# A searched-on instruction order: 110 further seeds for the planner of an attention, gated-mixer and token-mixer kernel

## The chip, the core and the metric

The kernel runs on one core of a Trainium2 chip. The metric is the device time of one launch in microseconds (us); lower is better. Engines are named as the profile names them: PE (TensorE; PEld are its weight loads), ACT (ScalarE), DVE (VectorE), POOL (GpSimd), SP (SyncE, which issues nearly all DMAs).

## The reference

Three stages follow each other, all in fp32, for 4 batches of 448 tokens with 768 features.

```python
q_n, k_n = rmsnorm(q, g_q), rmsnorm(k, g_k)          # 12 heads of 64
scores = q_n @ k_n.T / 8 ;  attn = exp(scores - max) ;  attn /= attn.sum() + 1e-9
x = attn @ v                                          # [4, 448, 768]
h = relu(x @ w_in) ;  u, v = halves of h              # 2 x 512
v_n = (v - mean) / sqrt(var + 1e-6)
x = (u * (w_spatial @ v_n + b_spatial)) @ w_out       # mixes over tokens
u = x + (relu(x.T @ w_tok1) @ w_tok2).T               # 448 -> 256 -> 448 over tokens
out = u + relu(u @ w_ch1) @ w_ch2                     # 768 -> 1536 -> 768
```

## The kernel before

**What runs when.** The 48 heads are taken as 24 pairs. For one pair, `Attention.slot` loads q and k (`load`), scales them on POOL (`scale`, output tile `raw`), turns them with PE (`transposed`), multiplies them (`scores`, PSUM tile `sc`), takes the row maximum on DVE (`nm`) and the exponential on ACT (`e`), turns `e` with PE (`turned`, PSUM tile `tp`, copied to `et`) and multiplies it with v (`values`, PSUM tile `av`). The row sums go another way: DVE adds 1e-9, inverts and transposes them (`divisors`, tiles `ring` and `rows`), SP writes them to DRAM (`over_d<-rows`) and reads them back spread over 64 partitions each (`over<-over_d`). DVE multiplies `av` with `over`, ACT rounds the product to its high part and POOL takes the low part (both in tile `xp`). A batch has six pairs, and when its six `xp` are there, `moe` computes the mixer: `vps` (v, six `xp` by w_in), `ups` (u), `sps` (over tokens), `xps` (w_out). Its weights come through DRAM; ACT, DVE, POOL and SP prepare them on the way (`word`, `wpart`, `wv`, `wu_d`, `stage`, `ws`). After the last batch come the token mixer (`h1ps`, `u_ps`, transposes of `x`) and the channel mixer in seven products each way (`h2ps`, `o_ps`).

Most matmuls take the operands as a high and a low fp32r part and run three passes. In the first eight pairs the scores take fp32 whole (`sc<-whole`), later three fp32r passes (`sc<-kt,qt`).

**What sets the order.** Nothing is issued while the loops run. `Plan.add` records each operation with its operands, a cost and its dependencies. At the end `Plan.issue` lays all recorded operations out by a list scheduler, `Plan.place`: on each engine the ready operation of the lowest weight goes first, with the PSUM banks given out as they come free, and the operations are then issued engine by engine in the order of the starts that it found. The weights come from eight rounds forward and back. They are then changed by a list of seeds:

```python
for seed in NUDGES:
    weight = nudged(weight, seed, engines)
start, span, bank = self.place(prev, succ, lag, weight, (opens, closes, users))
```

`nudged` turns a seed into a place in the program (modulo `NUDGED`, 4000), a reach, a size and a kind (all engines or one), and adds to the weights of the operations around that place a pseudo-random amount. So a seed moves no more than some operations against their neighbours; what is computed, with which tiles, stays. Which bank a PSUM tile takes follows the order as well. Before the change the list holds 228 seeds, all with the form 300xxxxx.

Nearly every instruction carries line L464, the helper that issues it, so that rows are told apart by their tiles.

Of the kernel before, what the change touches and what calls it, by code (L numbers as in the profile page):

```python
# [152 lines left out]
class Plan:  # L153
# [341 lines left out]
)  # L495
ENGINES = "gpsimd", "scalar", "sync", "tensor", "vector"
IDLE, SPARE, PACE = 1500, 200, 546
# [1179 lines left out]
```

## Time and profile before

| | us |
|---|---|
| median of three runs | 848.97 |
| lowest, highest | 847.46, 849.27 |
| the profiled execution | 847.23 |
| its span, first to last instruction | 845.2 |
| PE busy in the span | 833.1 |
| DVE, ACT, POOL busy | 674.7, 526.7, 344.6 |

The profiled execution took 2.0 us more than its span, and 1.74 us less than the median of the three runs. Sums below are made against its span, and their differences are then put to the median. A matmul's end in the trace is modelled and matmuls overlap, so a busy PE need not be one at its best pace; starts are what is measured.

### The profile page before, as it was taken

How to read it: one execution, taken by the hardware profiler on the slowest of the kernel's cores; microseconds unless marked ns; L12 is line 12 of the kernel's file. 1: busy time of each engine (PE TensorE's matmuls, PEld its weight loads, DVE VectorE, ACT ScalarE, POOL GpSimd, SP SyncE). 2: the span in 40 equal slices, each digit the busy share in tenths (PEclk: the TensorE clock that was granted, in tenths of full speed). 3: DMA queues.
4: the chain of work that ended last, by engine and by line, in shares of the span. 5: the costliest groups of instructions: out<-in, count | busy, mean ns of one | idle time of the engine just before them, and what ended most of it. 6: DMA issues, size and time to landing. Idle time of an engine off the chain costs nothing.

```text
span 845.2 us, 16488 instructions
## 1 busy us (share of the span) xinstructions
PE 833.1 (99%) x5530; PEld 700.4 (83%) x5530; DVE 674.7 (80%) x1340; ACT 526.7 (62%) x1268; POOL 344.6 (41%) x431
## 2 busy tenths in 40 slices
PE   7999999999999999999999999999999999999998
PEld 5454567777678876787799999999999999999998
DVE  6899899886787778787475677988889876998863
ACT  6999899897776878766343565554345654343331
POOL 2457555663445524242152222525331018515460
PEclk9999999999999999999999999999999999999999
DMA  6656676766765866466968787667555635742441
GB/s 170 161 160 185 177 232 184 236 169 170 241 184 144 216 171 196 124 180 194 331 201 247 234 275 252 220 197 221 156 175 175 214 123 161 226 140 84 140 142 66
DMA packets 158532, 157.94 MB, mean 187 GB/s; under 512 B 79216, under 2 KB 141616, under 8 KB 158448
## 3 DMA queue, kind: packets, MB, share of 16 engines
q1 hardware_dynamic: 157984, 156.86, 62.1%
q8 instruction: 44, 0.72, 0.4%
q14 instruction: 40, 0.33, 0.1%
q10 hardware_dynamic: 464, 0.03, 0.0%
HBM read 117.95 MB, written 38.88 MB: 186 GB/s over the span
## 4 chain that ended last, share of the span: by engine, by line
PE 82%; ACT 9%; DMA 3%; DVE 3%; issue 1%; SPq 1%; POOL 0%; ACTq 0%; POOLq 0%; DVEq 0%
PE o_ps L464 18%; PE h2ps L464 18%; PE xps L464 7%; PE ups L464 7%; PE av L464 6%; PE vps L464 5%; PE tp L464 5%; PE sc L464 4%; PE sps L464 4%; ACT e L464 4%; PE h1ps L464 4%; PE u_ps L464 3%; ACT et L464 2%; ACT sq L464 1%; DMA raw<-in_k_dram 1%
## 5 line engine op out<-in xcount | busy, mean ns | idle before, releaser
L464 PE MATMUL h2ps<-op,w 128*128 128x448 f32 x756 | 154.1, 366 | 0.0
L464 PEld LDWEIGHTS o_ps<-w,op 128*128 128x128 f32 x900 | 154.0, 188 | 0.0
L464 PE MATMUL o_ps<-w,op 128*128 128x384 f32 (+1 forms) x900 | 153.9, 332 | 0.0
L464 PEld LDWEIGHTS h2ps<-op,w 128*128 128x128 f32 x756 | 141.6, 188 | 11.2
L464 ACT ACTIVATE e<-sc,nm 112x448 f32<-112x448 f32 x184 | 121.7, 692 | 5.5 <-DVE nm L464 5.3
L464 DVE TENSOR_REDUCE nm<-sc 112x1 f32<-112x448 f32 x192 | 110.2, 615 | 8.0 <-PE sc L464 7.3
L464 ACT ACTIVATE op<-c 128x768 fp32r<-128x768 f32 x49 | 41.5, 847 | 83.7 <-PE o_ps L464 77.3
L464 POOL TENSOR_TENSOR src<-src 128x384 f32<-128x384 f32 x48 | 61.2, 1284 | 73.4 <-DMA src<-c_d 56.1
L464 PEld LDWEIGHTS tp<-ident,e 64*128 64x128 f32 (+2 forms) x1120 | 55.5, 139 | 27.4 <-ACT e L464 9.5
L464 ACT ACTIVATE et<-tp 128x448 f32<-128x448 f32 (+1 forms) x144 | 72.7, 560 | 4.9 <-PE tp L464 4.5
L464 DVE TENSOR_SCALAR word<-word 128x256 f32<-128x256 f32 (+5 forms) x132 | 60.5, 462 | 18.4 <-ACT word L464 17.3
L464 DVE SCALAR_TENSOR_TENSOR word<-raw,word 128x256 uint32<-128x256 uint32 (+2 forms) x132 | 71.2, 541 | 1.8
L464 POOL TENSOR_TENSOR u<-u,o 128x384 f32<-128x384 f32 x28 | 40.5, 1464 | 68.4 <-ACT o L464 38.9
L464 PE MATMUL tp<-ident,e 48*128 48x48 f32 (+2 forms) x1120 | 65.4, 232 | 1.2 <-ACT e L464 0.8
L464 PE MATMUL ups<-xp,wu 128*128 128x448 f32 x288 | 65.9, 368 | 0.0
L464 DVE TENSOR_TENSOR op<-c,op 128x768 fp32r<-128x768 f32 x49 | 54.6, 1115 | 10.3 <-ACT op L464 10.3
L464 PE MATMUL av<-et,v 128*64 128x448 f32 x288 | 61.1, 550 | 1.4 <-ACT e L464 0.9
L464 PEld LDWEIGHTS ups<-xp,wu 128*128 128x128 f32 x288 | 53.7, 188 | 6.4 <-ACT e L464 0.7
L464 DVE TENSOR_TENSOR c<-c,h2ps 128x448 f32<-128x448 f32 x84 | 49.7, 613 | 8.4 <-PE h2ps L464 8.2
L464 PE MATMUL xps<-wo,g 128*128 128x384 f32 x288 | 55.1, 340 | 0.0
L464 PE MATMUL sc<-kt,qt 64*112 64x448 f32 x384 | 52.9, 384 | 0.0
L464 PE MATMUL vps<-wv,xp 128*128 128x512 f32 x216 | 52.8, 397 | 0.0
(146 smaller groups left out, 1595.1 us busy)
## 6 DMA issues: line engine op xcount, KB each, us to landing
src<-c_d SPq DMA_DIRECT2D x132, 192.0 KB
wu<-wu_d SPq DMA_DIRECT2D x16, 768.0 KB
wo<-wo_d SPq DMA_DIRECT2D x16, 768.0 KB
raw<-in_moe_w_ch_dram SPq DMA_DIRECT2D x36, 256.0 KB
raw<-in_moe_w_ch_dram SPq DMA_DIRECT2D x24, 384.0 KB
raw<-in_q_dram SPq DMA_DIRECT2D x48, 112.0 KB
over<-over_d SPq DMA_DIRECT2D x48, 112.0 KB
u<-u_d SPq DMA_DIRECT2D x28, 192.0 KB
```

The lines of the kernel that those rows point to most:

```text
L464: getattr(getattr(self.nc, op.engine), fn)(*args, **kwargs)
```

## The change

One constant is longer: 110 seeds of the form 530xxxxxx stand behind the 228 old ones, from `530000073` to `530024960`. Everything else is the same text. The core of the diff:

```diff
-    30049953, 30050321, 30050423, 30050564, 30051641, 30053077, 30053387, 30053718,
+    30049953, 30050321, 30050423, 30050564, 30051641, 30053077, 30053387, 30053718, 530000073, 530000138, 530000164,
...
+    530017980, 530020788, 530021112, 530023085, 530023723, 530024223, 530024960,
 )
```

Each engine issues the same instructions as before, in the same number; only their order differs. On PE the two orders are the same up to 74 us of the trace of before, and again from 513 us on. Between them they differ most from 80 to 160 us and from 400 to 470 us, while from 180 to 400 us few rows move. SP's order differs from the first DMAs on.

PE, in the trace of before from 80.3 to 86.4 us: `tp<-ident,raw` are the transposes of the pair whose q and k POOL has just scaled; `stage` belongs to w_spatial. Before:

```order
L464 MATMUL tp<-ident,e 128x112 x14
L464 MATMUL av<-et,v_864 64x448 x2
L464 MATMUL tp<-ident,raw 128x112 x8
L464 MATMUL tp<-ident,stage 128x112 x3
L464 MATMUL sc<-whole 112x448 x2
```

And with the change:

```order
L464 MATMUL av<-et,v_864 64x448 x6
L464 MATMUL sc<-whole 112x448 x2
L464 MATMUL tp<-ident,e 128x112 x14
L464 MATMUL tp<-ident,raw 128x112 x4
L464 MATMUL av<-et,vrest 64x448 x2
L464 MATMUL sc<-whole 112x448 x2
L464 MATMUL tp<-ident,raw 128x112 x4
```

The eight transposes of `raw` now stand in two fours, with an `av` pair and a `sc` pair between them.

POOL, the same place; the two `raw<-raw,ry` are what those transposes wait for. Before:

```order
L464 TENSOR_TENSOR wv<-word,wv 128x512
L464 TENSOR_SCALAR ra<-ss 112x16
L464 CAST xr<-xp 128x128
L464 TENSOR_TENSOR xp<-over,xp 128x448
L464 TENSOR_TENSOR wv<-word,wv 128x512
L464 TENSOR_TENSOR rz<-ry 112x16
L464 CAST xr<-xp 128x128
L464 TENSOR_TENSOR rz<-rz,ra 112x16
L464 TENSOR_SCALAR rz<-rz 112x16
L464 TENSOR_TENSOR ry<-ry,rz 112x16
L464 TENSOR_TENSOR wpart<-wpart 128x256
L464 TENSOR_TENSOR raw<-raw,ry 112x512 x2
```

And with the change:

```order
L464 CAST xr<-xp 128x128
L464 TENSOR_SCALAR ra<-ss 112x16
L464 TENSOR_TENSOR rz<-ry 112x16
L464 TENSOR_TENSOR rz<-rz,ra 112x16
L464 TENSOR_TENSOR xp<-over,xp 128x448
L464 TENSOR_SCALAR rz<-rz 112x16
L464 TENSOR_TENSOR wv<-word,wv 128x512
L464 TENSOR_TENSOR ry<-ry,rz 112x16
L464 TENSOR_TENSOR raw<-raw,ry 112x512
L464 TENSOR_TENSOR wpart<-wpart 128x256
L464 TENSOR_TENSOR raw<-raw,ry 112x512
```

One `wv`, one `xr` and the `wpart` no longer stand ahead of the first `raw`.

PE again, from 93.4 to 105 us: the last `av` of the first batch's sixth pair, and the first `vps`, which need the six `xp`. Before:

```order
L464 MATMUL av<-et,vrest 64x448 x2
L464 MATMUL tp<-ident,e 128x112 x4
L464 MATMUL vps<-wv,xp 128x512 x5
L464 MATMUL tp<-ident,e 128x112 x3
L464 MATMUL vps<-wv,xp 128x512 x7
L464 MATMUL tp<-ident,e 128x112 x7
L464 MATMUL sc<-whole 112x448 x2
L464 MATMUL tp<-ident,raw 128x64 x14
L464 MATMUL sc<-whole 112x448 x2
L464 MATMUL av<-et,v_1310 64x448 x6
L464 MATMUL vps<-wv,xp 128x512 x12
```

And with the change:

```order
L464 MATMUL tp<-ident,e 128x112 x11
L464 MATMUL vps<-wv,xp 128x512 x5
L464 MATMUL tp<-ident,e 128x112 x3
L464 MATMUL vps<-wv,xp 128x512 x2
L464 MATMUL av<-et,vrest 64x448 x2
L464 MATMUL sc<-whole 112x448 x4
L464 MATMUL vps<-wv,xp 128x512 x10
L464 MATMUL tp<-ident,e 128x112 x6
L464 MATMUL vps<-wv,xp 128x512
```

The first accumulation of `vps` (18 matmuls, the last three of which read the sixth pair's `xp`) now ends ahead of the next pair's `av`; before, it ended behind it. The last of the ten and the one before it read the high part of the sixth `xp`, the single one behind the six transposes its low part.

SP, the DMAs around the sixth pair's divisors (`over_d_73`), in the trace of before from 88.7 to 97.5 us. Before:

```order
L464 DMA over_d_72<-rows 8x32
L464 DMA wu_d_60<-wpart 256x1x256
L464 DMA raw<-in_moe_w_in_dram 128x2x256
L464 DMA wu_d_61<-wpart 256x1x256
L464 DMA over_d_73<-rows 8x32 x3
L464 DMA over_d_73<-rows 8x16
L464 DMA over<-over_d_72 64x448 x2
L464 DMA vrest<-in_v_dram 64x64
L464 DMA raw<-in_moe_w_in_dram 128x2x256
L464 DMA over<-over_d_73 64x448 x2
```

And with the change:

```order
L464 DMA over_d_72<-rows 8x32
L464 DMA wu_d_60<-wpart 256x1x256
L464 DMA v_1316<-in_v_dram 128x3x64
L464 DMA vrest<-in_v_dram 64x64
L464 DMA raw<-in_moe_w_in_dram 128x2x256
L464 DMA over_d_73<-rows 8x32 x2
L464 DMA over_d_73<-rows 8x16
L464 DMA over_d_73<-rows 8x32
L464 DMA over<-over_d_72 64x448 x2
L464 DMA wu_d_61<-wpart 256x1x256
L464 DMA raw<-in_q_dram 64x7x64
L464 DMA over<-over_d_73 64x448 x2
```

Between the fifth and the sixth pair's divisors eleven issues have become twelve.

## Rows read from the trace of the kernel before

**Rows 1.** The page: the span, PE's busy share, the granted clock in 40 slices.

```profile
span 845.2 us, 16488 instructions
PE 833.1 (99%) x5530; PEld 700.4 (83%) x5530; DVE 674.7 (80%) x1340; ACT 526.7 (62%) x1268; POOL 344.6 (41%) x431
...
PEclk9999999999999999999999999999999999999999
```

**Rows 2.** Busy time by stage: length, engines (instructions), granted clock, DMA share, GB/s.

```profile
60.00:100.00 40.00, 38.58 (x242) 21.20 (x242) 36.69 (x89) 37.20 (x110) 26.77 (x40) 1.00 0.64 181
100.00:180.00 80.00, 79.38 (x664) 58.30 (x660) 73.19 (x184) 70.59 (x201) 47.99 (x76) 1.00 0.72 205
180.00:400.00 220.00, 219.92 (x1899) 167.77 (x1898) 169.29 (x414) 168.07 (x460) 86.71 (x139) 1.00 0.63 181
400.00:480.00 80.00, 80.00 (x422) 73.10 (x421) 46.56 (x103) 31.97 (x70) 25.82 (x23) 1.00 0.78 256
480.00:537.00 57.00, 56.95 (x352) 54.58 (x351) 45.81 (x80) 34.63 (x68) 19.91 (x14) 1.00 0.75 251
537.00:845.00 308.00, 305.27 (x1648) 293.98 (x1646) 256.31 (x367) 131.62 (x221) 111.80 (x86) 1.00 0.53 162
```

**Rows 3.** Groups by shape: the up-projection's matmuls (busy us, mean ns, idle before).

```profile
L464 PE MATMUL h2ps<-op,w 128*128 128x448 f32 x756 | 154.1, 366 | 0.0
```

**Rows 4.** PE in order of time, 80 to 85 us: start, us, [idle before <-releaser].

```profile
80.29 1.68 PE L464 MATMUL tp<-ident,e 112*128 112x112 f32 x14
...
83.59 0.60 PE L464 MATMUL tp<-ident,raw 112*128 112x112 f32 x4 [0.73 <-POOL raw L464]
84.59 0.60 PE L464 MATMUL tp<-ident,raw 112*128 112x112 f32 x4 [0.40 <-POOL raw L464]
```

**Rows 5.** POOL in order of time, 73 to 85 us.

```profile
73.61 1.28 POOL L464 TENSOR_TENSOR wv<-word,wv 128x512 fp32r<-128x512 f32 x1
...
80.07 0.29 POOL L464 CAST xr<-xp 128x128 fp32r<-128x128 f32 x1
...
81.81 0.73 POOL L464 TENSOR_TENSOR wpart<-wpart 128x256 fp32r<-128x256 f32 x1 [0.50 <-ACT wpart L464]
82.50 2.04 POOL L464 TENSOR_TENSOR raw<-raw,ry 112x512 f32<-112x512 f32 x2
```

**Rows 6.** The chain that ended last, 96 to 101 us: start, us, what.

```profile
96.91 3.66 DMA over<-over_d
```

**Rows 7.** All engines in order of time, 95 to 103 us.

```profile
95.07 0.54 SPq L464 DMA_DIRECT2D vrest<-in_v_dram  x1
...
96.12 1.85 PE L464 MATMUL vps<-wv,xp 128*128 128x512 f32 x7
...
97.81 0.83 PE L464 MATMUL tp<-ident,e 112*128 112x112 f32 x7
...
98.58 1.01 PE L464 MATMUL sc<-whole 64*112 64x448 f32 x4
...
99.42 0.60 PE L464 MATMUL tp<-ident,raw 64*128 64x64 f32 x14
...
99.85 0.96 PE L464 MATMUL sc<-whole 64*112 64x448 f32 x4
...
100.66 0.62 DVE L464 TENSOR_TENSOR over<-av,over 128x448 f32<-128x448 f32 x1 [0.50 <-DMA over<-over_d]
...
101.32 0.58 ACT L464 ACTIVATE xp<-over 128x448 fp32r<-128x448 f32 x1 [0.73 <-DVE over L464]
101.34 2.48 PE L464 MATMUL av<-et,v 128*64 128x448 f32 x12 [0.53 <-DVE over L464]
...
101.97 1.38 POOL L464 TENSOR_TENSOR xp<-over,xp 128x448 fp32r<-128x448 f32 x1 [1.62 <-ACT xp L464]
```

**Rows 8.** Waits by engine: us in total, times, longest.

```profile
PEld av L464 <- issue: 30.6, 125, 0.7
```

**Rows 9.** Busy time at the end, columns as in rows 2.

```profile
840.00:850.00 10.00, 2.27 (x21) 2.10 (x19) 0.71 (x2) 0.00 (x0) 0.00 (x0) 0.88 0.10 34
```

10 rows, old and new, of the table NUDGES are left out of this document.

## Prediction

> **What bounds the kernel now.** I read the page first, then the busy time by stage, then PE in order of time where the order changes, and behind each wait the engine or DMA that ended it.
>
> The page says that PE is busy for 833.1 of 845.2 us at a clock that stands at nines in all 40 slices [rows 1]. So nothing but PE's own time and its 12 us of idleness can give anything back. The stages say where [rows 2]. From 537 us on PE does the channel mixer without a gap, and its order there is the same in both kernels; the 756 matmuls of `h2ps` take 154.1 us together, 0.204 us apiece [rows 3]. These 308 us stay. From 180 to 537 us PE idles 0.13 us in all (0.08, 0.00 and 0.05 in the three stages) [rows 2]. Between 60 and 180 us it idles 2.04 us (1.42 and 0.62) while DVE and ACT are busy for 92 and 93% from 60 to 100 us. The reader is to see that an order of instructions can win two things here: about 2 us of visible idleness at 60 to 180 us, and the joints between matmuls of different forms, which hide inside PE's busy time. Up to 74 us PE's order is unchanged.
>
> **The change, part by part.** No instruction is added or removed, so each term is a wait or a joint. The sum is made against the profiled execution, 847.23 us for a span of 845.2.
>
> *The `raw` transposes at 83 us.* PE waits 0.73 and 0.40 us for POOL's two scalings, 1.13 us together [rows 4]. With the change a `wv` (1.28 us), an `xr` (0.29 us) and a `wpart` (0.73 us, with 0.50 us of idleness ahead of it) no longer stand ahead of POOL's first scaling [rows 5]: it can start 2.8 us earlier, against a wait of 0.73. What was put behind it is not late: the `wv` is of the mixer's first weights, wanted by `vps` 10 us later. The second four transposes moreover have an `av` and a `sc` pair in front of them now. I count both waits as gone: **-1.13**, with bounds -1.13 and 0. By itself this is only a lead that PE gains at 85 us; the next place decides whether it keeps it.
>
> *The sixth `xp` at 99 us.* Before, PE meets the pair's `over` late, at the next `av`, which takes the PSUM bank that DVE's product frees, and waits 0.53 us [rows 7]. DVE's product waits for the DMA that brings `over`: issued at 96.91, landed 3.66 us later at 100.57 [rows 6]. From there the product on DVE and the rounding on ACT end at 101.32 + 0.58 = 101.90, which is 1.33 us behind the landing [rows 7]. With the change the ninth of the ten `vps` needs that high part directly. When does PE come there? At 98.58 the old order had done all that the new one puts ahead, but for two `sc` pairs (98.58 to 99.42 is 0.84 us each) and three `vps` (96.12 to 97.81 is seven, so 0.24 each), and it had done seven transposes more (97.81 to 98.58, 0.77) [rows 7]: 98.58 + 1.68 + 0.72 - 0.77 = 100.21, or 99.08 with the lead. So PE waits from 99.08 for landing + 1.33, and against the old course (100.21, and the 0.53 us later) the stretch up to here costs landing - 99.41. If the landing comes forward by the whole lead, to 99.44, that is +0.03. The single `vps` behind the six transposes needs POOL's low part, at 101.97 + 1.38 = 103.35, 1.45 us behind the high one, where PE has two `vps` and six transposes to do, 0.48 + 0.66 us [rows 7]: +0.31 more. Together **+0.3** for the whole stretch from 74 to 105 us, the lead already in it. The bounds: if the landing comes by 97.75 nothing waits, and -1.13 - 0.53 = -1.66 remains; if it keeps its old time and the one more issue on SP comes on top (0.54 us as the `vrest` took [rows 7]), it is at 101.11, +1.70 and with the low part +2.0. I take the whole lead as moved, since the divisors hang on scores that PE reaches earlier by the lead; DVE's transpose of `rows` comes earlier on its engine as well, and the twelfth issue on SP speaks the other way.
>
> By the Trainium skill, DMA: Bandwidth & Descriptors, Anatomy of one DMA, a DMA has a fixed cost of about 2.0 us and moves 436 KB in each further us. The page fits that for POOL's software queue; worked out for a half of `over` of 115 KB it is an estimate of 2.26 us, so a landing 1.4 us earlier, and this term would come to -1.1 with the low part. The trace has 3.66 us for the same transfer, and the measurement decides.
>
> *The joints.* In PE's order the full array, the half rows (`sc`, transposes of 64 or 48 rows) and the half columns (`av`) follow each other 136 times before and 133 times with the change, counted over the whole order. No row prices a joint alone. The nearest is the weight load of `av`, which waits 125 times for nothing that the profile shows, 0.24 us on average and 0.7 at the longest [rows 8]. Three fewer: **-0.7**, bounds 0 (a load that waits while the last matmul still streams costs PE nothing) and -2.1.
>
> *The rest.* From 105 to 180 us many rows move, but PE idles only 0.62 us from 100 to 180, and 0.53 of that is the wait above [rows 2, 7]; from 400 to 480 it idles not at all [rows 2]. There is nothing to win; a new wait could come, and each `xp` and `vn` chain is a candidate. I take 0, and give it 0.6 us to either side, as much as PE now idles in the first of these stretches. SP's order in the first microseconds changes among loads that all precede the same work: 0.
>
> Sum: +0.3 - 0.7 = -0.4 us. The profiled execution would take 846.8 us; the median of runs stands 1.74 us above it, and I move it by the same: 848.97 - 0.4 = **848.6 us**. That is inside the 0.2% (1.7 us) below which a measurement of this kernel can't tell a change from none.
>
> **The rivals.**
>
> *Everything is covered: faster.* `over` lands early enough, by 97.75, so that no `vps` waits: -1.66, and -0.7 for the joints, -2.4 us, 846.6; with the joints at their longest 845.2. For it: POOL's scaling lost 2.8 us of other work ahead of it [rows 5], and DVE's transpose of `rows` may have lost as much on the way to `over`. The three runs of before also differ by 1.8 us, and an order that suffers less from whatever lengthens two of them would win part of that. Against it: the landing would have to come 2.8 us earlier while one more DMA stands ahead of it.
>
> *The new `vps` wait is paid in full: slower.* The landing stays at 101.11, PE stands behind the ninth `vps` for high and low part: +2.0 us, and the joints give nothing, 851.0. It decides from a landing of about 100.8 on: 100.8 - 99.41 + 0.31 is 1.7 us. For it: the engine that waits is PE, whose queue is strictly this order, and the bank that the wait holds back stands in front of the next pair's transposes. Against it: the chain starts from work that comes earlier.
>
> *The clock drops: slower.* The granted clock is 1.00, so 2.4 GHz, in each stage where the order moves [rows 2], and its only lower slice is the idle end with 0.88 [rows 9]. If a tenth of the 38.58 us of PE work from 60 to 100 us ran at 1.2 GHz it would cost 3.9 us more, 852.9. For it: the change puts fourteen and eleven short transposes in a row, and PE waits at a new place. Against it: fourteen stand in a row at 80 us before, too [rows 4], PE waits 2.04 us in these stages as it is, and the trace grants the full clock throughout.
>
> That the new seeds change nothing is excluded by the orders shown.
>
> **How the numbers follow.** No change that can be told: 0.44, the forecast. All covered: 0.36. The `vps` wait in full, or another of its kind at 120 to 145 us: 0.17. The clock: 0.03. Faster by over 0.2% (below 847.3) 0.36, within 0.2% 0.44, slower 0.20. The range goes from 845.2, the faster rival at its bound, to 851.2, the slower one with 0.2 us for the unread rest; the clock's case is left out, and what lies beyond the bounds. The forecast alone holds from 847.3 to 850.7.
>
> **What would show it.** In the trace of the changed kernel: (1) PE's `raw` transposes at 83 us without a wait for POOL. (2) A wait of PE inside the first `vps` at about 99 us, ended by ACT `xp`, of about 1.7 us, and none any more at the `av` that follows. (3) The landing of `over`: at 99.4, or 97.8, or 101. (4) 537 us as the start of `h2ps`, give or take half a microsecond; the 308 us behind it unchanged. (5) 1.00 as the granted clock throughout. The prediction is wrong if `h2ps` starts more than 1.7 us earlier or later, or if the stretch from 180 us on changes by more than 1 us, where I see nothing to win or lose.

## The result, and the profile after

The changed kernel takes **852.42 us** (median of six runs, 851.34 to 855.36), the kernel before on the same chip 848.51 us: a ratio of **1.0051, interval 1.0033 to 1.0070**. That is slower, by 3.9 us or 0.5%; 848.6 was forecast and the range ended at 851.2. The profiled execution took 852.83 us, its span is 851.0. The two profiles differ by more (5.8 us of span) than the medians, since the profiled execution of before lies 1.3 us under its median.

The page of the changed kernel, first the span and the busy times, then the granted clock in 40 slices, answering to [rows 1]:

```profile
span 851.0 us, 16471 instructions
...
PE 836.7 (98%) x5530; PEld 704.0 (83%) x5530; DVE 670.0 (79%) x1340; ACT 525.4 (62%) x1268; POOL 341.4 (40%) x431
...
PEclk9999999999999999999999999999999999999999
```

The group of `h2ps` reads as in [rows 3], 154.1 us for 756 matmuls, 0.204 us apiece. The stages, answering to [rows 2] (the last two borders moved by the 6 us that PE is behind there):

```profile
60.00:100.00 40.00, 39.06 (x228) 21.26 (x227) 37.97 (x89) 37.44 (x111) 25.37 (x41) 1.00 0.61 180
100.00:180.00 80.00, 77.97 (x634) 57.49 (x634) 71.19 (x177) 68.08 (x193) 46.10 (x74) 1.00 0.71 201
180.00:400.00 220.00, 217.38 (x1910) 164.41 (x1911) 170.59 (x413) 167.82 (x466) 88.66 (x140) 1.00 0.61 179
400.00:480.00 80.00, 79.69 (x415) 72.54 (x414) 40.54 (x105) 29.01 (x68) 22.67 (x23) 1.00 0.81 254
...
543.00:851.00 308.00, 305.11 (x1648) 293.86 (x1646) 254.63 (x367) 131.60 (x220) 110.66 (x85) 1.00 0.53 162
```

From 60 to 100 us PE idles 0.94 us, where it was 1.42: the part on which the prediction spent its working has become better. From 100 to 180 us it idles 2.03 us (0.62 before), from 180 to 400 us 2.62 us (0.08 before), from 400 to 480 us 0.31 (0.00). Apart from the wait at 101 us those three stages were put down as zero. The first row below is what is left of the waits at `raw`; the five behind it make up 3.5 of the 5.0 us that PE idles from 100 to 480 us, in PE's order of time:

```profile
83.38 0.57 PE L464 MATMUL tp<-ident,raw 112*128 112x112 f32 x4 [0.43 <-POOL wpart L464]
...
101.31 0.73 PE L464 MATMUL vps<-wv,xp 128*128 128x512 f32 x2 [0.53 <-ACT xp L464]
...
168.00 0.86 PE L464 MATMUL sc<-kt,qt 64*112 64x448 f32 x5 [1.03 <-ACT et L464]
...
188.83 1.28 PE L464 MATMUL sc<-kt,qt 64*112 64x448 f32 x6 [1.06 <-DVE over L464]
...
302.80 1.49 PE L464 MATMUL xps<-wo,g 128*128 128x384 f32 x7 [0.55 <-DMA wo<-wo_d]
...
453.79 0.80 PE L464 MATMUL xps<-wo,g 128*128 128x384 f32 x3 [0.31 <-ACT g L464]
```

For whole orders a **lag** serves below: how much later than in the profile of before PE stands at a place up to which both have started the same matmuls (the order differs, the matmuls do not). For the change it is +0.5 us at 70, -0.8 at 88, +0.3 at 97, +0.8 at 131, +1.1 at 148, +1.5 at 150, +2.9 at 170, +4.4 at 200, +5.3 at 300, +5.7 at 400, +6.3 at 500. So the loss comes in steps, not evenly. Ahead of 130 us a gain of 1.3 us and losses of 1.6 us nearly cancel; the two largest steps, 1.5 us each, belong to the waits at 168 and 188 us.

Not every loss shows as a wait. From 88 to 93 us the change loses 0.9 us although PE is busy throughout. A `sc` pair there takes 1.51 us from its start to the start of the next group, where the old order takes 0.94, and the next pair, at 91.54, takes 1.25 for 0.95. In the kernel before two matmuls of such a pair start at the same time; in the change the second one starts 0.58 and 0.32 us behind the first, right after ACT's `e` and `et` have ended, to which the profile puts it down. First the change, then the kernel before:

```profile
88.30 1.58 PE L464 MATMUL sc<-whole 64*112 64x448 f32 x4
89.81 0.89 PE L464 MATMUL tp<-ident,e 112*128 112x112 f32 x7
```
```profile
88.23 1.01 PE L464 MATMUL sc<-whole 64*112 64x448 f32 x4
89.17 1.70 PE L464 MATMUL tp<-ident,e 112*128 112x112 f32 x14
```

Loads stand in the chains that lead to the waits at 168 and 188 us. ACT, in order of time:

```profile
154.58 0.58 ACT L464 ACTIVATE sq<-raw 128x448 f32<-128x448 f32 x1 [0.92 <-DMA raw<-in_q_dram]
...
158.71 0.42 ACT L464 ACTIVATE wpart<-wpart 128x256 fp32r<-128x256 f32 x1 [1.81 <-DVE wpart L464]
...
166.84 0.52 ACT L464 ACTIVATE g<-tg 128x384 fp32r<-128x384 f32 x1 [0.38 <-POOL tg L464]
167.27 0.24 ACT L464 ACTIVATE rest<-tg 128x64 fp32r<-128x64 f32 x1
167.42 1.30 ACT L464 ACTIVATE et<-tp 128x448 f32<-128x448 f32 x3
```

The square `sq` of a pair's q and k starts at 154.58; in the kernel before the same instruction starts at 147.24. Only 0.92 of these 7.3 us is a wait for the load. The three `et`, whose PSUM banks PE wants at 168.00, stand behind a `g` that waits for POOL. The chain that ended last comes there from a load of k, issued at 160.28 and landed 2.34 us later, through POOL's `raw` and `tg`; that the late square leads to it as well is not shown. SP issued the load that the square waits for at 147.98, directly behind the 768 KB of `wu`; in the kernel before at 142.90, ahead of it. The change, then SP and ACT of the kernel before:

```profile
146.12 0.63 SPq L464 DMA_DIRECT2D raw<-in_k_dram  x1
146.80 0.61 SPq L464 DMA_DIRECT2D v<-in_v_dram  x1
147.45 0.48 SPq L464 DMA_DIRECT2D wu<-wu_d  x1
147.98 0.63 SPq L464 DMA_DIRECT2D raw<-in_q_dram  x1
...
179.06 1.95 SPq L464 DMA_DIRECT2D raw<-in_k_dram  x3
181.05 1.12 SPq L464 DMA_DIRECT2D v<-in_v_dram  x2
182.27 0.43 SPq L464 DMA_DIRECT2D x_d<-xo  x1
182.79 2.96 SPq L464 DMA_DIRECT2D over<-over_d  x2
```
```profile
142.90 0.63 SPq L464 DMA_DIRECT2D raw<-in_q_dram  x1
```
```profile
147.24 0.62 ACT L464 ACTIVATE sq<-raw 128x448 f32<-128x448 f32 x1
```

The last of SP's rows of the change is the reading back of `over` for 188 us: the first of two at 182.79, the second at 185.16; in the kernel before at 179.33 and 179.83. PE's wait there ends with DVE's product, which waits for that read:

```profile
188.15 0.62 DVE L464 TENSOR_TENSOR over<-av,over 128x448 f32<-128x448 f32 x1 [1.72 <-DMA over<-over_d]
```

### The profile page after: what moved, and what is told of

Read it like the earlier page. It is cut to its first block, busy times and chain, and to the rows that moved or that the text cites. A ratio compares the mean times of both kernels' runs of the same rounds, so it can differ in the third digit from the quotient of the medians.

```text
span 851.0 us, 16471 instructions
## 1 busy us (share of the span) xinstructions
PE 836.7 (98%) x5530; PEld 704.0 (83%) x5530; DVE 670.0 (79%) x1340; ACT 525.4 (62%) x1268; POOL 341.4 (40%) x431
## 4 chain that ended last, share of the span: by engine, by line
PE 67%; DMA 10%; ACT 10%; DVE 6%; SPq 4%; issue 2%; POOL 1%; ACTq 0%; DVEq 0%; POOLq 0%
PE o_ps L464 18%; PE h2ps L464 18%; PE xps L464 5%; PE ups L464 5%; SPq L464 4%; PE h1ps L464 4%; PE u_ps L464 4%; ACT e L464 3%; PE sps L464 3%; PE tp L464 3%; PE av L464 3%; DMA wu<-wu_d 2%; PE vps L464 2%; PE sc L464 2%; DMA wo<-wo_d 2%
## 5 line engine op out<-in xcount | busy, mean ns | idle before, releaser
L464 PE MATMUL h2ps<-op,w 128*128 128x448 f32 x756 | 154.1, 366 | 0.0
L464 DVE TENSOR_SCALAR word<-word 128x256 f32<-128x256 f32 (+5 forms) x132 | 57.7, 439 | 21.1 <-ACT word L464 19.9
```

The source lines that it names most:

```text
L464: getattr(getattr(self.nc, op.engine), fn)(*args, **kwargs)
```

## Experiments

Times are ratios to the kernel before, run beside each on the same chip, with their 95% intervals; the change itself has 1.0051 (1.0033 to 1.0070). All kernels but those with an edit of a queue issue one of the two orders, or pieces of both; none leaves work out.

### One queue exchanged, and two groups of loads moved

The theories: (1) SP's order costs; (2) the order on the compute engines costs; (3) a stretch of half clock costs, which the profile of the change shows at 18 to 21 us.

```diff
-        for i in sorted(range(len(ops)), key=lambda i: (start[i], i)):
+        for i in self.mixed_order(start, made[1 - BASE][0], best[2], closes, prev):
```

The rest of the edit is left out here. `mixed_order` keeps each engine's order of one plan, but takes SP's (all of it, or its first part) from the other, or moves the operations named ahead of another one.

e1, SP of before under the change: 

> The changed kernel on PE, ACT, DVE and POOL, with SP's queue of DMA issues in the order of before. Theory 1 (the order of SP's queue costs: the loads of k at 160 us, the read of over at 183 us, the start): the places at 160 to 190 us and the start give back some 3.4 us, the lead of 0.8 us at the raw transposes stays, so 847.5 to 849.5 us, ratio to the kernel before 0.999 to 1.001. Theory 2 (the order on the compute engines costs, SP's is carried along): 851 to 853 us, ratio 1.003 to 1.006.

e2, SP of the change under before: 

> The reverse: the kernel before on PE, ACT, DVE and POOL, with SP's queue in the order of the change. Theory 1: the late issues cost here too, 851 to 853 us, ratio 1.003 to 1.006. Theory 2: 848 to 849 us, ratio 0.999 to 1.001. If both this and its counterpart are slower than before, it is the fit of the two that costs, and neither order alone.

e3, only SP's start: 

> The changed kernel, with only the first part of SP's queue (the DMAs of the first microseconds, before the first batch's mixer) in the order of before. Theory 1: the 0.5 us that PE was behind at 60 us goes, and nothing else: 851.5 to 852.3 us, ratio 1.0035 to 1.0045; PE is level with before at 60 us (0.2 us either way). Theory 3 (the stretch of half clock at 18 to 21 us costs what its 3.4 us of PE work would save at full clock, 1.7 us): with the loads as before the stretch goes and the time falls to about 850.5 us, ratio 1.0025.

e4, loads moved: 

> The changed kernel with eight DMA... six issues moved within SP's queue and nothing else: the three loads of k ahead of the weights' write that stood before them at 152 us, the last write of the fourth pair's row sums two issues earlier, and the two reads of over ahead of that slot's loads of k. Theory 1: the waits of 1.03 us at 168 us and of 1.06 us at 188.8 us go, with the 0.4 to 0.5 us each that PE works slower around them: 849 to 850.5 us, ratio 1.001 to 1.0025; PE is behind before by about 1.5 us at 160 us and by no more than 2.5 us at 200 us, where the change has 4.4. Theory 2: as the change, 851.5 to 853 us; the two waits come back elsewhere.

Measured: e1 **1.0272** (1.0251 to 1.0293), e2 **1.0312** (1.0283 to 1.0342), e3 **1.0097** (1.0081 to 1.0114), e4 **1.0061** (1.0042 to 1.0081). Both exchanges cost five to six times what the change does, so no queue's order is good or bad by itself: it fits the other queues or it doesn't. The stage from 100 to 180 us of e1 shows it, where PE is busy for 69.92 us and the clock is down:

```profile
100.00:180.00 80.00, 69.92 (x503) 49.70 (x505) 62.11 (x159) 57.97 (x161) 36.70 (x57) 0.94 0.60 171
```

e3 shows two things. PE's lag at 60 us stays (0.4 us), so SP's start did not make it; and a stretch of lower clock stays as well (0.97 granted from 0 to 60 us, as in the change), only earlier: 0.81 from 14 to 18 us and 1.00 from 18 to 21. So e3 does not test theory 3; that falls by the profile of the change itself, where the lag is +1.5 us at 20 us and back at 0.0 at 30 us. Why e3 is 4 us slower than the change is only partly seen, in the last section. e4 refutes theory 1 as put. With the loads of k earlier the wait at 168 us stays and is longer (1.45 us), and PE loses 2.4 us between 160 and 170 us in its profile, more than in the change; the wait at 188 us is gone, but a wait of 0.86 us for `wo` has come at 199 us.

### The orders joined in time

So all engines and SP were changed over together, at one time of the plan.

```diff
-            start, span, bank = self.place(prev, succ, lag, weight, (opens, closes, users))
+            start, span, bank = self.merged_order(made, prev, succ, lag, (opens, closes, users))
```

`merged_order` takes every operation that the first order starts before the border, then the rest in the second order, and gives out the PSUM banks anew along it; in the trace of e6 the queues change over between 150 and 157 us. What the banks given out anew do by themselves no run tells; e5 and e14, level with the kernel before, leave them little. Theory 4: each place costs where its own order stands. Theory 5: a different start is carried along.

e5: 

> All engines and SP in the order of the change up to about 93 us of the trace, from there on in the order of before (banks given out along the joined order). The two runs in which only SP's order was exchanged have shown that no engine's order can be judged alone, so the orders are now joined in time, all engines at once. Theory 4 (each place costs where its own order stands): the gain at the raw transposes stays and the rest is as before, so PE is 0.1 to 0.5 us ahead of before at 95 us and stays so, 847.5 to 848.5 us, ratio 0.9985 to 1.000. Theory 5 (the different start is carried along and meets the later waits out of step): the losses from 150 us on come back although the order there is that of before, 851 to 853 us.

e6: 

> As the run before, with the orders joined at about 150 us: the first vps, the second batch's pairs and its mixer's first half in the order of the change, the places at 168 and 188 us in that of before. Theory 4: the drift of 1.4 us at 150 us and none after it, 849.5 to 850.5 us, ratio 1.001 to 1.0025. Theory 5: 852 us or more, as the change.

e7: 

> Joined at about 200 us: the places at 168 and 188 us are those of the change, what follows is before's. Theory 4: the drift of 4.4 us at 200 us and none after it, 851.2 to 852.5 us, ratio 1.0035 to 1.005. If the time is level with before, the loss arises behind 200 us, against both.

e8: 

> The reverse: before up to about 150 us, the change from there on. Theory 4: only what the change loses behind 150 us, 5.84 - 1.46 = 4.4 us, 851.5 to 853.5 us, ratio 1.004 to 1.006. Theory 5: without the changed start nothing is out of step, 848 to 849 us.

e12: 

> The order of before up to 200 us, that of the change from there on: what the places at 300 and 450 us cost by themselves. From the profile of the change 5.84 - 4.38 = 1.5 us: 849.2 to 850.2 us, ratio 1.001 to 1.0025. If the load of q at 148 us is all of it (theory 6 at its strongest), 848 to 848.7 us, ratio 1.0005 at most.

e14: 

> All engines in the order of the change up to 130 us, then of before. If the loss from 92 to 150 us is the late load of q at 148 us (theory 6), this costs nothing yet: ratio 0.9995 to 1.0007. If it is the first vps at 99 us and what hangs on it (the slower rival of the prediction), 1.0015 to 1.003.

e18: 

> The order of before up to 150 us and from 200 us on, that of the change in between alone. By the difference of the two runs that start with before (1.0044 joined at 150 us, 1.0017 joined at 200 us): ratio 1.002 to 1.0035. If the shares do not add up because a late stretch only costs where the earlier one has used up the slack: 1.000 to 1.001.

| the change's order | ratio | interval |
|---|---|---|
| up to 92 us (e5) | 1.0001 | 0.9990 to 1.0012 |
| up to 130 us (e14) | 1.0004 | 0.9993 to 1.0016 |
| up to 150 us (e6) | 1.0026 | 1.0015 to 1.0037 |
| up to 200 us (e7) | 1.0036 | 1.0023 to 1.0048 |
| everywhere | 1.0051 | 1.0033 to 1.0070 |
| from 150 us on (e8) | 1.0044 | 1.0027 to 1.0062 |
| from 200 us on (e12) | 1.0017 | 1.0007 to 1.0028 |
| only 150 to 200 us (e18) | 1.0011 | 1.0000 to 1.0023 |

The times follow theory 4 and not theory 5: nothing measurable up to 130 us, then 0.0022 for the order from 130 to 150 us (e6 less e14), 0.0011 for that from 150 to 200 us, 0.0017 for that behind it. With e14 that is 0.0054, the change has 0.0051. The shares themselves are rough: the intervals of e14 and e6 touch, and that of e18 begins at 1.0000. e18 also came out lower than the 1.002 to 1.0035 worked out for shares that add up, and e8 has more than e18 and e12 together, so the stretches need not be independent.

As to the place, theory 4 does not hold: a stretch of order need not be paid for where it stands. In e6 all queues follow the order of before from about 157 us on, and yet in its profile the lag goes from +0.6 us at 160 to +3.4 at 170, where theory 4 forecast none. Four waits of PE make up 1.87 us of that, two of them:

```profile
161.69 2.48 PE L467 MATMUL av<-et,v 128*64 128x448 f32 x12 [0.67 <-ACT tg L467]
...
168.45 0.85 PE L467 MATMUL sc<-kt,qt 64*112 64x448 f32 x5 [0.57 <-DVE et L467]
```

So what the order up to 150 us sets up is carried along for 10 to 20 us and paid there, and the share of a stretch below is that of its order, wherever it is paid.

e5 also shows what the gain at `raw` is worth. PE is ahead by 0.7 us at 88 us and 0.5 us behind at 96: the two `sc` pairs take as long as in the change, 1.51 and 1.25 us. Then, with before's order behind it, `over` lands no earlier in its profile (101.72, for the 100.57 of [rows 6]), and PE waits there for 0.89 us, where it was 0.53 [rows 7]. First the chain that ended last, then PE:

```profile
98.28 3.44 DMA over<-over_d
...
101.82 0.64 DVE over L467
```
```profile
102.50 2.48 PE L467 MATMUL av<-et,v 128*64 128x448 f32 x12 [0.89 <-DVE over L467]
```

The lead is gone before that landing, and the landing adds to the loss.

### The load of q at 148 us

Theory 6: this load is the first cause of the losses up to 200 us. Theory 7: it is one of many. The order of SP's issues, written as a diff:

```diff
-SP: ..., raw(k), v, wu, raw(q), wo_d, ...
+SP: ..., raw(k), v, raw(q), wu, wo_d, ...
```

e9 is the diff in the change, e11 in the order joined at 150 us, e16 the same with this load and that of k at 142 us. e10 does the reverse in the kernel before: the load goes back behind `v`, `raw(k)` and `wu`, which is three issues and not five.

e9: 

> The changed kernel with two neighbours of SP's queue exchanged: the load of half a q (112 KB), which stands directly behind the 768 KB of wu at 147.5 us, goes ahead of it. Theory 6 (a load of q is late: in the change ACT's first square of that pair starts at 154.6 us for 147.2 before, ACT, DVE and POOL fall 2 us behind PE, SP's next weight load finds its buffer taken, and the waits of PE at 168 and 188 us follow): the square starts 2.5 to 4 us earlier and PE loses 1.5 us less or better between 150 and 200 us; with 1.5 to 2.9 us back, 849.5 to 851 us, ratio 1.0015 to 1.0035. Theory 7 (the order from 150 us on costs by itself, the load is only one of many): 852 to 853 us, ratio 1.0045 or more.

e10: 

> The cost put into the kernel before: the same load of half a q moved five issues back in SP's queue, behind wu (and k, two of v, which stood behind it), nothing else. Theory 6: the square comes late by 3 to 6 us, PE loses 1.5 to 3 us between 160 and 200 us, 849.7 to 851.5 us, ratio 1.002 to 1.004. Theory 7: hidden by the pairs in hand, 847.5 to 848.7 us, ratio 0.9995 to 1.0005.

e11: 

> The joined order of the change up to 150 us and of before from there, which took 1.0026 times before, with the load of half a q ahead of wu. Theory 6: the loss behind 150 us is that load's, ratio 1.000 to 1.0015, 848 to 849.3 us. Theory 7: 1.0025 as without the exchange; then the loss lies in the rest of the order from 92 to 150 us.

e16: 

> The joined order of the change up to 150 us (1.0026 times before; 1.0016 with the load of q one place earlier), with two loads of that pair moved ahead to 142 us. Theory 6: ACT's square starts by 150 us instead of 154, ratio 0.9995 to 1.001. If the rest of the order from 92 to 150 us costs: 1.0015 to 1.0025.

Measured: e9 1.0051 (1.0032 to 1.0071), **e10 1.0044 (1.0030 to 1.0059)**, e11 1.0016 (1.0007 to 1.0026), e16 1.0021 (1.0010 to 1.0032). e10 is the clearest of all runs: one load, issued at 145.63 instead of 142.90, costs the kernel before about as much as the whole change. It lands 5.58 us after its issue; in the kernel before it was there by 147.24, when ACT took it without a wait, so in 4.34 us at most. ACT stands for it, DVE's `ss` for ACT's square, DVE's `over` behind `ss`, and PE for `over`. First the load in the chain that ended last, then ACT and PE:

```profile
145.63 5.58 DMA raw<-in_q_dram
```
```profile
151.37 0.58 ACT L467 ACTIVATE sq<-raw 128x448 f32<-128x448 f32 x1 [2.83 <-DMA raw<-in_q_dram]
```
```profile
153.18 0.68 PE L467 MATMUL sps<-ws,vn 128*128 128x448 f32 x2 [1.59 <-DVE over L467]
```

The run does not tell the later issue from the slower landing. The reverse does not hold. In e16 the load no longer holds ACT up, yet the square starts at 152.51, because ACT itself comes there late, with other work ahead of it (its rows from 138 us to there show 0.74 us of idle time in all):

```profile
151.91 0.66 ACT L467 ACTIVATE e<-sc,nm 112x448 f32<-112x448 f32 x1
152.42 0.24 ACT L467 ACTIVATION_READ_ACCUMULATOR e<-sc,nm 112x1 f32 x1
152.51 0.61 ACT L467 ACTIVATE sq<-raw 128x448 f32<-128x448 f32 x1
153.81 0.58 ACT L467 ACTIVATE sq<-raw 128x448 f32<-128x448 f32 x1 [0.69 <-DVE ss L467]
```

Theory 6 is right on the price of such a lateness and too strong on its share: by e11 and e16 it is 0.0005 to 0.0010 of the 0.0026, within the intervals perhaps nothing. In e9's profile PE loses only 0.2 us between 160 and 170 us (1.5 in the change), but 2.1 us between 200 and 230 us, where the change lost nothing: the loss moved on.

### The read of x at 450 us, and all moves together

In the order of the change ACT's `xh`, which waits for `x` from DRAM, stands ahead of a `g` that PE wants. These are the rows of e12 (the change from 200 us on), first the chain that ended last, then ACT, then PE:

```profile
440.08 9.03 DMA x<-x_d
```
```profile
449.19 0.84 ACT L467 ACTIVATE xh<-x 128x768 fp32r<-128x768 f32 x1 [1.85 <-DMA x<-x_d]
449.94 0.51 ACT L467 ACTIVATE g<-tg 128x384 fp32r<-128x384 f32 x1
```
```profile
450.50 0.81 PE L467 MATMUL xps<-wo,g 128*128 128x384 f32 x3 [1.53 <-ACT g L467]
```

In the kernel before a `g` goes first (446.42) and `xh` starts at 446.99 without a wait. e13 puts the order on ACT right in e12's kernel, e15 puts that and the early loads of q and k into the change, e17 adds e4's moves. The order of ACT's instructions, written as a diff:

```diff
-ACT: ..., xh, g, rest, word, g, rest, ...
+ACT: ..., g, rest, xh, word, g, rest, ...
```

e13: 

> The order of before up to 200 us and of the change from there (1.0017 times before), with one edit on ACT at 449 us: the first g and its rest go ahead of xh, which waits for the read of x from DRAM. Theory 8 (ACT's in-order wait for a transfer is the loss behind 200 us): PE's wait for g at 450 us (1.5 us in the profile) goes, ratio 1.000 to 1.001. Theory 9 (spread over many places): 1.0015 to 1.002.

e15: 

> The changed kernel (1.0051 times before) with both edits: two loads of the pair's q and k issued some 5 us earlier, at 142 us, and g ahead of xh at 450 us. Theories 6 and 8: 2 to 4 us come back, ratio 1.001 to 1.003. If the loss only moves on to the next place, as with the exchange of two neighbours: 1.004 to 1.005.

e17: 

> The changed kernel with all moves together: the two loads of q and k at 142 us, g ahead of xh at 450 us (these two gave 1.0033), and the k loads, the last write of the row sums and the two reads of over earlier (which alone gave 1.0061, no better than the change). If the later loads are waits of their own behind the first one: another 1 to 1.5 us, ratio 1.0015 to 1.0025. If moving them only pushes other transfers back: 1.003 to 1.005.

Measured: e13 1.0015 (1.0001 to 1.0030), e15 **1.0033** (1.0021 to 1.0044), e17 1.0044 (1.0031 to 1.0057). In e13's profile the wait at 450 us is gone (PE goes through `xps` there without a wait), and so are 1.8 us between 440 and 450 us; its twelve runs spread from 847.7 to 853.1 us and their ratio can't tell it from e12. Theory 8 is right for the place and not shown for the time; the ratio is the one that theory 9 forecast. e15 is some 1.5 us faster than the change, with intervals that overlap, and lies between its two forecasts. e17 is not faster than e15: of five moves the last three gave nothing, as in e4. No joined or mended order beat the kernel before; e5 and e14 equal it.

## Why the prediction was wrong

**The `raw` transposes (-1.13).** Right in kind and nearly in size: one wait of 0.43 us is left of 1.13, and from 70 to 88 us PE goes from 0.5 us behind before to 0.8 us ahead of it. POOL's first scaling starts at 81.09 for 82.50, 1.4 us earlier and not 2.8: POOL waits for DVE and ACT in front of it (1.06 and 1.92 us).

**The sixth `xp` at `vps` (+0.3 for the stretch).** Right in the sum, and by luck. The wait came where it was forecast, inside the first `vps` and by ACT's `xp`, and the `av` that follows has none. DVE's product starts at 100.03 as the second half of `over` lands, about 0.5 us later than the 99.44 taken:

```profile
100.03 0.62 DVE L464 TENSOR_TENSOR over<-av,over 128x448 f32<-128x448 f32 x1 [0.61 <-DMA over<-over_d]
```

PE goes on at 101.31. Its own wait is 0.53 us and not the 1.7 forecast, as it comes to the ninth `vps` at 100.78 and not at 99.08. Of these 1.7 us, 0.5 is the lag that PE had at 70 us already, and 0.9 went in the two `sc` pairs at 88 and 91 us, which the prediction did not look at. POOL's low part, counted as +0.31, costs no wait. So the lead was lost in another place, and the wait came out shorter by about as much. The lag goes from +0.5 us at 70 to +0.8 at 131, and e14 measures the whole of it, with the joints, as 1.0004: the sum of -0.4 us is inside its interval (-0.6 to +1.4 us).

**The joints (-0.7).** The weight loads that were taken as their price did not become fewer: 126 waits of 30.3 us in all for the 125 of 30.6 in [rows 8]. No run separates the joints otherwise; they are part of what e14 finds to be nothing.

```profile
PEld av L464 <- issue: 30.3, 126, 0.7
```

**The clock.** As forecast at 1.00 in every stage behind 60 us. Ahead of it the sign "throughout" does not hold: 0.50 from 18 to 21 us. That stretch is made good by 30 us, as said above, and is not the loss.

**"The rest: 0".** This is the step that failed. The text said that from 105 us on there was nothing to win, allowed a new wait 0.6 us to either side and named the `xp` and `vn` chains as candidates. The lack of idle time on PE was read as slack for the order, where it only says that nothing is left to be won. The order from 130 to 150 us cost about 1.9 us (0.0022), that from 150 to 200 us 0.9, and that behind 200 us, where few rows move until 400 us, 1.4. The sign that the prediction named for being wrong has come: the first `h2ps` starts at 540.20 for 534.11, and the stretch behind 180 us loses 2.9 us in the profile. (The 537 us that it gave for this start was the border of a stage; before, too, the first `h2ps` is earlier.) First the change, then the kernel before:

```profile
540.20 0.65 PE L464 MATMUL h2ps<-op,w 128*128 128x448 f32 x2
```
```profile
534.11 0.65 PE L464 MATMUL h2ps<-op,w 128*128 128x448 f32 x2
```

**SP's order (0).** Part of the same step. Only SP's start was judged and found harmless, which e3 bears out for the lag at 60 us. SP's order at 142 to 148 us was neither read nor priced, and a load that stands behind `wu` there costs the kernel before 3.7 us (e10).

**The rivals.** The slower rival gave 851.0 for a `vps` wait in full "or another of its kind at 120 to 145 us"; the size is near, the place is not `vps`. It had 0.17, and the faster rival, with the wrong sign, 0.36. The clock's rival, 852.9, comes nearest to the 852.42 measured, but its cause is absent: the granted clock is 1.00 in the stages that it named.

What stays open: how the 0.0022 of the order from 130 to 150 us divides beyond the load of q, and what the 0.0017 behind 200 us consists of. ACT's square comes 5 us late even with its data in place (e16), so ACT's own order may have a share; no run isolates it.

## What to carry to other kernels

That PE has no idle time left is no sign of slack in the order. Here PE was 99 to 100% busy, the reordering won 1.3 us by 88 us and had lost it again by 97, and the waits behind late chains at 168 and 188 us cost a microsecond each. A busy share hides waits, too: compare the starts of the same group in both profiles, as at the `sc` pairs. Price the stretches in which SP's loads move past a large transfer, not only those in which PE waits now. To find where a reordering loses, join the two orders in time, all queues at once; exchanging one queue showed here only that the queues fit together (1.0272 and 1.0312). And read a place in several profiles before calling it the cause: a single wait that was removed came back a place later in e4 and e9.

## What the runs showed of the hardware

**A transfer behind a large one.** In e12 the second of two reads of `x`, 192 KB each, landed 9.03 us after its issue, behind two loads of 768 KB of `wo` that SP had issued in the 4.4 us ahead; in e10 a load of 112 KB directly behind the 768 KB of `wu` took 5.58 us; the reading back of `over`, 112 KB a half, took 2.84 to 3.66 us where none of that size had been issued for 10 us. By the Trainium skill, DMA: Bandwidth & Descriptors, Anatomy of one DMA (a fixed cost of about 2.0 us and 436 KB in each further us, which the page fits for POOL's software queue, while SP issued these), a read of 192 KB is an estimate of 2.45 us. The trace has more than three times that, and the measurement decides: the issue alone does not say when data lands.

**The clock falls behind a wait.** In e3 PE is busy for 2.55 of 4 us from 165 to 169 us, and then, fully busy again, it is granted 0.5, so 1.2 GHz, until about 172 us:

```profile
165.00:169.00 4.00, 2.55 (x41) 1.95 (x40) 2.79 (x7) 3.62 (x11) 3.37 (x5) 1.00 0.85 243
169.00:169.50 0.50, 0.50 (x4) 0.29 (x2) 0.50 (x2) 0.50 (x3) 0.44 (x2) 0.65 1.03 372
169.50:172.00 2.50, 2.50 (x8) 2.20 (x8) 2.40 (x6) 1.99 (x7) 0.62 (x1) 0.50 0.96 329
172.00:175.00 3.00, 3.00 (x15) 2.76 (x14) 1.81 (x5) 2.44 (x9) 2.33 (x5) 0.91 0.47 138
```

With the part that is not granted times the length of each row that is 1.7 us on top of a wait of 1.45 us, and as much as this profile of e3 lags behind that of the change at 500 us (8.0 for 6.3 us); how often it comes in e3's other runs is not known. At the same place, with a wait of 1.03 us, the change kept the full clock.

**The spread of one order.** The profiles of e5 and e18, whose orders are nearly before's, lag 3.7 and 4.1 us at 500 us, while their medians are 0.1 and 0.9 us above before; the profiled executions lie 2.3 and 1.7 us above those medians. The runs of the kernel before themselves spread over 1.8 us here (847.46 to 849.27). So steps of a microsecond in one profile are within what a single order does from run to run, and only the medians above decide.
